# Stage 2 of an attention and expert kernel as two 64-row halves of the TensorE array, summed by VectorE

## The chip, the cores and the metric

The kernel runs on one core of one Trainium2 chip. The time is device microseconds of one execution; the kernel before took 500.78 us (median of 3 runs, 500.53 to 500.85). Engines are called PE (TensorE matmuls), PEld (TensorE's weight loads), DVE (VectorE), ACT (ScalarE) and SP (the engine that issues most DMAs).

## The reference

An attention with a small state (8 batches, 8 heads, 512 tokens and 32 state rows of 64 numbers) in both directions, and then a bilinear expert network over all 8 x 544 = 4352 rows:

```python
scores = scale * np.matmul(x, state.transpose(0, 1, 3, 2))
a = softmax(scores); xread = np.matmul(a, state)
scores2 = scale * np.matmul(state, x.transpose(0, 1, 3, 2))
a2 = softmax(scores2); sread = np.matmul(a2, x)
x = concat([xread, sread])          # 8 x 544 rows of 512
h = (x @ w1) * (x @ w2)             # 1024 wide
return (h @ w3) @ w_out             # 512 wide
```

## The kernel before, in words

A prologue turns the float64 weights into f32 and multiplies w3 by w_out once, so that the network's second half is a single product with `wo` (1024 x 512). Both factors of the large products are split into a high and a low fp32r part, and three products (low x high, high x high, high x low) stand for one f32 product.

For each batch there are two stages on PE:

- **Stage 1** (`stage1`, L297 to L311), 8 steps `ft` of 12 full-array matmuls of 512 columns (L306). Each step fills a pair of PSUM banks with x @ w1 and x @ w2 for 128 of the 1024 columns. `hidden` (L287) evacuates it: ACT copies one bank (L290), DVE multiplies it by the other (L291), ACT and DVE split the result into `g_hi` and `g_lo` (L96, L97).
- **Stage 2** (`stage2`, L320), 4 tiles `tt` of 128 tokens. Each sums 8 x 3 = 24 full-array matmuls (L316) into one bank; `store` (L326) lets ACT copy the bank to a tile `tmp` (L329) and then issues the output DMA from ACT's own queue (L331).

After the first stage 2 tile of batches 1 to 6 stand the **side steps** of the next batch (`side_steps`, L335): two weight products `w[0]`, `w[1]`, the score product, `read_state` of this batch (L242, and its scaling on DVE, L247), and two more weight products `w[2]`, `w[3]`. Weight and score products are the per-head matmuls at L146: 64 rows by 32 columns of the array, f32, eight places of the array one after the other. Each weight product is split into `sw_hi` (ACT, L96) and `sw_lo` (DVE, L97). Batch 7 has only `read_state` there. The softmax of the next batch runs on DVE and ACT meanwhile (L186 to L227).

At the end `state_rows` (L492) does the same network for the 256 state rows: 8 steps with pieces of w1 and w2 that ACT and DVE split on the way (`grp_z`), and 2 stage 2 tiles.

PSUM has eight banks. The pool `ps_o` holds two single banks (`bank()`), the pool `ps_2` three pairs (`two_banks()`); each request takes the buffer that was requested longest ago and waits until its last reader is done. Before the change the stage 2 tiles and `read_state` take single banks; stage 1, weight products and scores take pairs.

PE's and SP's instructions stand in the order in which the code issues them. ACT's and DVE's are ordered by the tile framework after the prologue, with `store` and `hidden` at high priority. Every engine works its own queue in order, and ACT's queue holds its casts and copies as well as its output DMAs.

Of the kernel before, what the change touches and what calls it, by code (L numbers as in the profile page):

```python
# [27 lines left out]
ALU = mybir.AluOpType  # L28
AX = mybir.AxisListType
P = 128  # L30
# [8 lines left out]
def attn_bilinear_kernel(  # L39
# [10 lines left out]
    nc = tc.nc  # L50
    B, _, NT, H, D = x_s.shape
    S = NT * P
    NP = H // 2
    NS = st.shape[3]
    KT = H * NS // P
    FT, DO = w34_k.shape[0], out.shape[2]
# [3 lines left out]
    PER = P // NS  # L60
# [23 lines left out]
    wo = {part: const.tile([P, FT, DO], F32R, name=f"wo_{part}") for part in ("hi", "lo")}  # L84
    const.tile([P, 32], F32, name="pad_1")

    def bank():
        return ps_o.tile([P, NF], F32, name="ps_o")

    def two_banks():  # L90
        return ps_2.tile([P, 2, NF], F32, name="ps_2")

    def split(hi, lo, src):

        return (
            nc.scalar.copy(out=hi, in_=src),  # L96
            nc.vector.tensor_tensor(out=lo, in0=src, in1=hi.bitcast(F32), op=ALU.subtract),  # L97
        )
# [51 lines left out]
    def load_x(b):  # L150
        sts[b] = att.tile([P, NP, NS], F32, name="st")
        nc.sync.dma_start(out=sts[b], in_=st[b])
        x_tiles[b] = att.tile([P, NP, S], F32, name="x_d", bufs=1)
        nc.sync.dma_start(out=x_tiles[b], in_=x_d[b])

    def load_tokens(b):
        token_tiles[b] = att.tile([P, NT, H, D], F32, name="x_s", bufs=1)
        nc.sync.dma_start(out=token_tiles[b], in_=x_s[b])
# [135 lines left out]
    def new_g():  # L294
        return [main.tile([P, NF], F32R, name=f"g_{part}", bufs=FT) for part in ("hi", "lo")]
# [17 lines left out]
    def project(ps, gs, tt, ft):  # L313
        g_hi, g_lo = (g[:, tt * P:(tt + 1) * P] for g in gs[ft])
        for k, (g, w) in enumerate(((g_hi, "lo"), (g_hi, "hi"), (g_lo, "hi"))):
            nc.tensor.matmul(  # L316
                ps[:, :DO], g, wo[w][:, ft, :], start=(ft == 0 and k == 0), stop=(ft == FT - 1 and k == 2)
            )

    def stage2(gs, tt, dests):  # L320
        ps = bank()
        for ft in range(FT):
            project(ps, gs, tt, ft)
        store(ps, dests)

    def store(ps, dests):  # L326
        o = main.tile([P, NF], F32, name="tmp", bufs=4)[:, :DO]
        with tc.high_priority():
            stored[:] = [nc.scalar.copy(out=o, in_=ps[:, :DO])]  # L329
        for (dest, first, n), queue in zip(dests, cycle((nc.scalar, nc.sync))):  # L330
            queue.dma_start(out=dest, in_=o[first:first + n])  # L331

# [2 lines left out]
    def side_steps(b):  # L335


        if b == B:
            return [[reads[b - 1]], [], [], []]
        scores, reads[b], a2 = attention_steps(b)  # L340
        w = sw_steps(b)
        softmax = scores()
        first = partial(islice, softmax, 3)
        if b == 1:
            def rest():

                with tc.issue_after(stored[0].ins):
                    yield from softmax

            return [[first], [reads[0], w[0], w[1]], [], [rest], [w[2], w[3]], []]  # L350

        product = partial(islice, softmax, 1)
        return [[w[0], w[1], product, reads[b - 1], w[2], w[3], lambda: softmax], [], [], []]

    def run(steps):
        for step in steps:
            for _ in step() or ():
                pass

    def batch_stage2(b, gs):  # L360
        side = side_steps(b + 1)
        for tt in range(NT):
            stage2(gs, tt, [(out[b, tt * P:(tt + 1) * P], 0, P)])
            run(side[tt])
        if b + 1 < B:
            load_tokens(b + 1)
        if b + 2 < B:
            load_x(b + 2)


    with tc.tile_pool(name="pro", bufs=2) as pro:
# [43 lines left out]
        gs, acc, early = [], [], range(2)  # L415
# [10 lines left out]
        pair = two_banks()  # L426
# [53 lines left out]
        for tt in range(NT):  # L480
            dests = [(out[0, tt * P:(tt + 1) * P], 0, P)]
            if tt in early:
                store(acc[tt], dests)
            else:
                stage2(gs, tt, dests)
            run(side[tt])
# [5 lines left out]
    def state_rows():  # L492
        n = B * NS

        sr = late.tile([P, NP, 2, n], F32R, name="grp_sr")
        split(sr[:, :, 1], sr[:, :, 0], sread)
        gs = []
        for ft in range(FT):
            quarter, c = divmod(ft * P, NQ)
            ps = two_banks()  # L500
            for i in range(2):
                wh, wl = (late.tile([P, NP * P], F32R, name=f"grp_z{q}", bufs=3) for q in range(2))
                as_w = lambda t: t.rearrange("p (j f) -> p j f", j=NP)
                split(as_w(wh), as_w(wl), w_sb[:, quarter, i, :, c:c + P])
                for kt in range(NP):
                    ks = slice(kt * P, (kt + 1) * P)
                    nc.tensor.matmul(ps[:, i], wh[:, ks], sr[:, kt], start=(kt == 0), stop=False)  # L507
                    nc.tensor.matmul(ps[:, i, :n], wl[:, ks], sr[:, kt, 1], start=False, stop=(kt == NP - 1))  # L508
            gs.append([g[:, :n] for g in new_g()])
            sums = main.tile([P, 2, n], F32, name="tmp", bufs=4)  # L510
            halves = ps.rearrange("p i (half n) -> p i half n", n=n)
            nc.scalar.copy(out=sums, in_=halves[:, :, 1])
            nc.vector.tensor_tensor(out=sums, in0=sums, in1=halves[:, :, 0], op=ALU.add)
            nc.vector.tensor_tensor(out=sums[:, 0], in0=sums[:, 0], in1=sums[:, 1], op=ALU.mult)
            split(*gs[-1], sums[:, 0])
        for tt in range(n // P):
            stage2(gs, tt, [(out[tt * PER + q, S:], q * NS, NS) for q in range(PER)])


    for b in range(1, B):  # L520
        gs = []
        for ft in range(FT):
            stage1(b, ft, gs)
        batch_stage2(b, gs)
    with tc.issue_after(last_split[0].ins), tc.issue_after(last_split[1].ins):
        state_rows()
# [44 lines left out]
```

## Time and profile before

| what | value |
|---|---|
| median of 3 runs | 500.78 us |
| span of the profiled execution | 498.4 us |
| PE busy | 492.3 us, 99% |
| PEld busy | 362.8 us, 73% |
| DVE busy | 285.7 us, 57% |
| ACT busy | 219.3 us, 44% |
| mean granted TensorE clock | 0.999 |

The span runs from the first to the last instruction of the profiled execution; that execution has no time of its own on record besides its span. Matmuls overlap in the pipeline, so the mean duration of one is longer than the distance from one to the next; the distance is read from the chain of work that ended last, as the length of a piece over its count. A plain f32 matmul of the code stands in the trace as two matmul records, an fp32r one as one. An entry like `[0.70 <-DVE sw_lo L97]` says that the engine sat idle for 0.70 us before the instruction and which one ended the wait. Of the groups by line, the columns are the count, the busy time in all, the mean of one in ns, and the idle time before them.

### The profile page before, as it was taken

The numbers are of one execution on the slowest core, as the hardware profiler recorded it, in microseconds if no ns is written. First come the engines' busy times: TensorE is split into PE (matmuls) and PEld (weight loads), VectorE is DVE, ScalarE is ACT, GpSimd is POOL, SyncE is SP. The second block draws the span as 40 slices with busy tenths as digits, with TensorE's granted clock in tenths as the row PEclk, the third lists the DMA queues.
The fourth block names the chain that finished last, engine by engine and source line by source line (L and its number), as shares of the span: only waits on it lengthen the run. The fifth ranks groups of instructions, "written<-read, shape, count | busy, mean of one in ns | idle before, by whom it ended". The sixth has DMA issues, their size and how long they took to land.

```text
span 498.4 us, 7562 instructions
## 1 busy us (share of the span) xinstructions
PE 492.3 (99%) x3054; PEld 362.8 (73%) x3054; DVE 285.7 (57%) x394; ACT 219.3 (44%) x325; POOL 0.2 (0%) x4
## 2 busy tenths in 40 slices
PE   8999999999999999999999999999999999999996
PEld 6444467767867886788678867886788678888885
DVE  5669896772539343934393539354934493530780
ACT  4777884443444244334333434243424342431650
POOL 0000000000000000000000000000000000000000
PEclk9999999999999999999999999999999999999999
DMA  8996962013400350035003500350035003301001
GB/s 343 364 380 237 364 264 33 11 47 80 181 22 19 79 189 23 20 79 188 21 27 76 185 22 27 77 184 22 26 78 183 22 26 78 93 24 49 21 1 42
DMA packets 52323, 52.41 MB, mean 105 GB/s; under 512 B 42304, under 2 KB 43328, under 8 KB 47680
## 3 DMA queue, kind: packets, MB, share of 16 engines
q1 hardware_dynamic: 47488, 43.27, 26.3%
q10 hardware_dynamic: 4800, 8.65, 4.6%
q8 instruction: 24, 0.39, 0.3%
q14 instruction: 11, 0.09, 0.1%
HBM read 38.27 MB, written 8.91 MB: 95 GB/s over the span
## 4 chain that ended last, share of the span: by engine, by line
PE 95%; DVE 2%; ACT 2%; DMA 1%; issue 0%; DVEq 0%
PE ps_o L316 38%; PE ps L306 35%; PE ps L146 7%; PE ps L507 3%; PE ps_o L402 3%; PE ps_o L389 3%; PE ps L389 3%; PE ps L508 2%; PE ps_o L242 1%; DMA raw<-in_w_k_dram 1%; ACT ulps L125 0%; ACT w_sb L117 0%; ACT wo_hi L96 0%; DVE w L133 0%; DVE work L204 0%; DVE wo_lo L97 0%
## 5 line engine op out<-in xcount | busy, mean ns | idle before, releaser
L316 PE MATMUL ps_o<-wo_lo,g_hi 128*128 128x512 f32 x272 | 107.0, 394 | 0.0
L316 PE MATMUL ps_o<-wo_hi,g_hi 128*128 128x512 f32 x272 | 106.0, 390 | 0.0
L316 PE MATMUL ps_o<-wo_hi,g_lo 128*128 128x512 f32 x272 | 105.9, 389 | 0.0
L306 PE MATMUL ps<-at_lo,sw_hi 128*128 128x512 f32 x256 | 100.1, 391 | 0.0
L306 PE MATMUL ps<-at_hi,sw_lo 128*128 128x512 f32 x256 | 99.6, 389 | 0.0
L306 PE MATMUL ps<-at_hi,sw_hi 128*128 128x512 f32 x256 | 99.6, 389 | 0.0
L291 DVE TENSOR_TENSOR tmp<-tmp,ps 128x512 f32<-128x512 f32 x64 | 43.9, 687 | 77.0 <-ACT tmp L290 76.9
L97 DVE TENSOR_TENSOR g_lo<-tmp,g_hi 128x512 fp32r<-128x512 f32 (+1 forms) x72 | 47.5, 661 | 41.7 <-ACT g_hi L96 41.6
L96 ACT CAST g_hi<-tmp 128x512 fp32r<-128x512 f32 (+1 forms) x72 | 43.1, 599 | 53.6 <-DVE tmp L291 48.8
L290 ACT COPY tmp<-ps 128x512 f32<-128x512 f32 x64 | 37.7, 589 | 62.8 <-PE ps L306 52.2
L316 PEld LDWEIGHTS ps_o<-wo_lo,g_hi 128*128 128x128 f32 x272 | 51.0, 188 | 18.0 <-issue 7.5
L316 PEld LDWEIGHTS ps_o<-wo_hi,g_lo 128*128 128x128 f32 x272 | 51.1, 188 | 10.8
L316 PEld LDWEIGHTS ps_o<-wo_hi,g_hi 128*128 128x128 f32 x272 | 51.1, 188 | 10.3
L97 DVE TENSOR_TENSOR sw_lo<-ps,sw_hi 128x1024 fp32r<-128x1024 f32 (+1 forms) x34 | 38.4, 1155 | 32.8 <-ACT sw_hi L96 32.8
L306 PEld LDWEIGHTS ps<-at_lo,sw_hi 128*128 128x128 f32 x256 | 48.1, 188 | 10.9 <-issue 1.1
L306 PEld LDWEIGHTS ps<-at_hi,sw_hi 128*128 128x128 f32 x256 | 48.1, 188 | 10.2 <-issue 0.2
L306 PEld LDWEIGHTS ps<-at_hi,sw_lo 128*128 128x128 f32 x256 | 48.1, 188 | 10.0
L329 ACT COPY tmp<-ps_o 128x512 f32<-128x512 f32 x34 | 19.8, 583 | 76.1 <-PE ps_o L316 76.1
L96 ACT CAST sw_hi<-ps 128x1024 fp32r<-128x1024 f32 (+1 forms) x34 | 31.7, 967 | 14.3 <-PE ps L146 14.2
L146 PE MATMUL ps<-w_sb,st 64*32 64x512 f32 (+1 forms) x544 | 31.6, 572 | 0.0
L402 PE MATMUL ps_o<-w_sb,w 128*128 128x512 f32 x64 | 28.5, 599 | 0.1
L402 PEld LDWEIGHTS ps_o<-w_sb,w 128*128 128x128 f32 x64 | 11.8, 190 | 15.9 <-issue 13.8
(65 smaller groups left out, 417.9 us busy)
## 6 DMA issues: line engine op xcount, KB each, us to landing
raw<-in_w_k_dram SPq DMA_DIRECT2D x8, 1024.0 KB, 6.6
x_d<-in_x_d_dram SPq DMA_DIRECT2D x8, 1024.0 KB, 7.1
raw<-in_w_dram SPq DMA_DIRECT2D x8, 1024.0 KB, 6.3
x_s<-in_x_s_dram SPq DMA_DIRECT2D x8, 1024.0 KB, 5.4
out_dram<-tmp ACTq DMA_DIRECT2D x32, 256.0 KB, 2.0
raw<-in_w3t_dram SPq DMA_DIRECT2D x4, 1024.0 KB, 7.2
a_t<-work SPq DMA_DIRECT2D x96, 32.0 KB, 1.9
sread<-turned SPq DMA_DIRECT2D x128, 4.0 KB, 1.7
```

The source lines that it names most:

```text
L96: nc.scalar.copy(out=hi, in_=src),
L97: nc.vector.tensor_tensor(out=lo, in0=src, in1=hi.bitcast(F32), op=ALU.subtract),
L146: nc.tensor.matmul(ps[j * NS:(j + 1) * NS, q], sts[b][rows, j], moving(rows, j), start=True, stop=True)
L290: nc.scalar.copy(out=a_sb[:, :n], in_=ps[:, 0, :n])
L291: nc.vector.tensor_tensor(out=a_sb[:, :n], in0=a_sb[:, :n], in1=ps[:, 1, :n], op=ALU.mult)
L306: nc.tensor.matmul(ps[:, i], w[:, kt, c:c + P], a[:, kt], start=(k == 0), stop=(k == 3 * KT - 1))
L316: nc.tensor.matmul(ps[:, :DO], g, wo[w][:, ft, :], start=(ft == 0 and k == 0), stop=(ft == FT - 1 and k == 2))
L329: stored[:] = [nc.scalar.copy(out=o, in_=ps[:, :DO])]
L389: nc.tensor.matmul(w34_ps[i][:, :DO], chunks[k][:, DO + i * P:DO + (i + 1) * P], w_out[k], start=(k == 0), stop=(k == FT - 1),)
L402: nc.tensor.matmul(w34_ps[i][:, :DO], w3s[i][:, k * P:(k + 1) * P], w_out[k], start=(k == 0), stop=(k == FT - 1))
L507: nc.tensor.matmul(ps[:, i], wh[:, ks], sr[:, kt], start=(kt == 0), stop=False)
L508: nc.tensor.matmul(ps[:, i, :n], wl[:, ks], sr[:, kt, 1], start=False, stop=(kt == NP - 1))
```

## The change

Stage 2 of batches 1 to 7 and of the state rows is computed by `stage2_rows`. Each of its matmuls becomes two: one over the upper 64 rows of the contraction (array rows 0 to 63), one over the lower 64. Both have all 128 columns. The two halves sum in two different banks, 24 matmuls into each. `store` lets ACT copy the first bank as before and then has DVE add the second to the copy; the DMA follows the add. Batch 0 keeps its stage 2. The banks come from `sums_of`: tiles 0, 2 and 3 of a batch take a pair of `ps_2`, tile 1 takes both single banks of `ps_o`; of the state rows' two tiles the first takes the single banks, the second a pair.

```diff
+    def stage2_rows(gs, tt, dests, sums):
+        for ft in range(FT):
+            g_hi, g_lo = (g[:, tt * P:(tt + 1) * P] for g in gs[ft])
+            for k, (g, w) in enumerate(((g_hi, "lo"), (g_hi, "hi"), (g_lo, "hi"))):
+                for r, ps in enumerate(sums):
+                    rows = slice(r * P // 2, (r + 1) * P // 2)
+                    nc.tensor.matmul(
+                        ps[:, :DO], g[rows], wo[w][rows, ft, :],
+                        start=(ft == 0 and k == 0), stop=(ft == FT - 1 and k == 2),
+                    )
+        store(sums[0], dests, sums[1])
+
-    def store(ps, dests):
+    def store(ps, dests, other=None):
         o = main.tile([P, NF], F32, name="tmp", bufs=4)[:, :DO]
         with tc.high_priority():
             stored[:] = [nc.scalar.copy(out=o, in_=ps[:, :DO])]
+            if other is not None:
+                nc.vector.tensor_tensor(out=o, in0=o, in1=other[:, :DO], op=ALU.add)
...
+    def sums_of(tt):
+        if tt == 1:
+            return bank(), bank()
+        pair = two_banks()
+        return pair[:, 0], pair[:, 1]
+
     def batch_stage2(b, gs):
         side = side_steps(b + 1)
         for tt in range(NT):
-            stage2(gs, tt, [(out[b, tt * P:(tt + 1) * P], 0, P)])
+            stage2_rows(gs, tt, [(out[b, tt * P:(tt + 1) * P], 0, P)], sums_of(tt))
             run(side[tt])
...
-            stage2(gs, tt, [(out[tt * PER + q, S:], q * NS, NS) for q in range(PER)])
+            stage2_rows(gs, tt, [(out[tt * PER + q, S:], q * NS, NS) for q in range(PER)], sums_of(1 - tt))
```

On ACT, this stands after the first stage 2 tile of batch 3 before the change, from that tile's copy to the cast of the next batch's `at_hi`. In brackets are the engines and DMA lanes that an instruction waits for.

```order
L329 COPY tmp<-ps_o 128x512 [waits PE_49,Activation_49]
L331 DMA out_dram<-tmp 128x512 [waits DMAHW6_49,Activation_49]
L96 CAST sw_hi<-ps_1987 128x1024 [waits PE_49]
L96 CAST sw_hi<-ps_2000 128x1024 [waits PE_49]
L96 CAST sw_hi<-ps_2075 128x1024 [waits PE_49]
L196 ACTIVATE e_2106,sum_2107<-ps_2013,m_2103 128x512 [waits DVE_49]
L196 ACTIVATE e_2106,sum_2107<-ps_2013,m_2103 128x512
L96 CAST sw_hi<-ps_2088 128x1024 [waits PE_49]
L207 ACTIVATE work<-work 128x1024 [waits DMAHW2_49,DMAHW5_49,DMAHW1_49,DVE_49]
L329 COPY tmp<-ps_o 128x512 [waits PE_49]
L331 DMA out_dram<-tmp 128x512 [waits DMAHW7_49,Activation_49]
L96 CAST at_hi<-work 128x1024 [waits DVE_49]
```

And after the change, at the same place (copy and DMA are at L343 and L347 there):

```order
L343 COPY tmp<-ps_2161 128x512 [waits PE_49,Activation_49]
L347 DMA out_dram<-tmp 128x512 [waits DMAHW6_49,DVE_49]
L96 CAST sw_hi<-ps_2214 128x1024 [waits PE_49]
L96 CAST sw_hi<-ps_2227 128x1024 [waits PE_49]
L96 CAST sw_hi<-ps_2302 128x1024 [waits PE_49]
L196 ACTIVATE e_2333,sum_2334<-ps_2240,m_2330 128x512 [waits DVE_49]
L196 ACTIVATE e_2333,sum_2334<-ps_2240,m_2330 128x512
L96 CAST sw_hi<-ps_2315 128x1024 [waits PE_49]
L207 ACTIVATE work<-work 128x1024 [waits DMAHW3_49,DMAHW4_49,DMAHW0_49,DVE_49]
L96 CAST at_hi<-work 128x1024 [waits DVE_49]
L343 COPY tmp<-ps_o 128x512 [waits PE_49,Activation_49]
L347 DMA out_dram<-tmp 128x512 [waits DMAHW1_49,DVE_49]
```

The first tile's DMA keeps its place ahead of the casts, but waits for DVE's add in place of ACT's own copy. The second tile's copy and DMA have moved behind the cast of `at_hi`. On DVE the first tile's add (L345) stands ahead of the `sw_lo` subtractions, and the adds of tiles two to four stand together behind the last step of the softmax (L227); in batch 7 they stand behind the split of the state rows (`grp_sr`).

On PE, this stands at the start of a batch's second stage 2 tile before the change (batch 3; `ps_o_2146` is the tile's bank, and the row ahead is the last of the side steps' per-head matmuls):

```order
L146 MATMUL ps_2_2088<-w_sb_90,st_1795 32x512 x7
L316 MATMUL ps_o_2146<-wo_lo_94,g_hi_1812 128x512 [waits Activation_49]
L316 MATMUL ps_o_2146<-wo_hi_93,g_hi_1812 128x512
L316 MATMUL ps_o_2146<-wo_hi_93,g_lo_1813 128x512
L316 MATMUL ps_o_2146<-wo_lo_94,g_hi_1832 128x512
L316 MATMUL ps_o_2146<-wo_hi_93,g_hi_1832 128x512
```

And after the change, at the same place; `ps_o_2373` takes the upper half's sum, `ps_o_2374` the lower half's (the 128x512 is the shape of the output, not of the weights):

```order
L146 MATMUL ps_2_2315<-w_sb_90,st_1997 32x512 x7
L334 MATMUL ps_o_2373<-wo_lo_94,g_hi_2014 128x512
L334 MATMUL ps_o_2374<-wo_lo_94,g_hi_2014 128x512 [waits DVE_49]
L334 MATMUL ps_o_2373<-wo_hi_93,g_hi_2014 128x512
L334 MATMUL ps_o_2374<-wo_hi_93,g_hi_2014 128x512
L334 MATMUL ps_o_2373<-wo_hi_93,g_lo_2015 128x512
L334 MATMUL ps_o_2374<-wo_hi_93,g_lo_2015 128x512
```

Every matmul has become two that follow each other. Before, the tile's first matmul waited for ACT's copy of the first tile; now the lower half's first one waits for DVE: its bank is the one that `read_state` used in the same batch and that the scaling (L247) reads. (Before, that was the bank of the third tile.)

## The prediction

> **What bounds the kernel now.** I read the page's busy times first, then the chain that ended last, then the timeline of one batch (the one from 365 to 416 us).
>
> ```profile
> PE 492.3 (99%) x3054; PEld 362.8 (73%) x3054; DVE 285.7 (57%) x394; ACT 219.3 (44%) x325; POOL 0.2 (0%) x4
> PE 95%; DVE 2%; ACT 2%; DMA 1%; issue 0%; DVEq 0%
> L316 PE MATMUL ps_o<-wo_lo,g_hi 128*128 128x512 f32 x272 | 107.0, 394 | 0.0
> ```
>
> TensorE (PE) is busy for 99% of the span and is 95% of the chain; stage 2 (L316) is one of its two large parts. Whatever PE loses or gains per matmul, or waits at a stage's edge, arrives at the end one for one. The 394 ns of a stage 2 matmul is a latency: matmuls overlap in the pipeline. The rate stands in the chain (columns: start, length, what, how many):
>
> ```profile
> 15.24 1.72 PE ps_o L389 x4
> 388.42 5.44 PE ps_o L316 x24
> 393.86 2.74 PE ps L146 x48
> 396.60 1.03 PE ps_o L242 x64
> 397.63 1.91 PE ps L146 x32
> 399.53 16.59 PE ps_o L316 x72
> 416.12 21.76 PE ps L306 x96
> 494.44 0.59 ACT tmp L329
> ```
>
> A full-array fp32r matmul of 512 columns costs 5.44/24 = 0.2267 us, in stage 2 as in stage 1 (21.76/96 = 0.2267). A plain f32 one (L389) costs 1.72/4 = 0.430 us.
>
> **Part 1: 720 full-array matmuls become 720 pairs.** Batches 1 to 7 have 7 x 4 tiles of 24 matmuls (672), the state rows 2 x 24 (48). Each becomes two matmuls of 64 rows and 128 columns. No row of this trace has that shape in fp32r. The nearest one is the per-head product (L146), 64 rows by 32 columns in f32, eight places of the array at once (first number: start):
>
> ```profile
> 394.25 0.15 PEld L146 LDWEIGHTS ps<-w_sb,st 64*32 64x32 f32 x8 [0.28 <-issue]
> 394.67 0.15 PEld L146 LDWEIGHTS ps<-w_sb,st 64*32 64x32 f32 x8 [0.28 <-issue]
> 395.10 0.15 PEld L146 LDWEIGHTS ps<-x_d,st 64*32 64x32 f32 x8 [0.28 <-issue]
> ```
>
> A round of eight comes every 0.43 us, exactly the 0.430 us of one f32 matmul on the whole array. So both row halves and all column groups run together, into two banks, and packing costs nothing; nor does it gain anything per round. I take the same for the pair: 0.2267 us, a change of 0. The bounds: 0.430/2 = 0.215 us, half of what an f32 record takes for the same 512 columns, as the best a pair could do (720 x -0.0117 = -8.4 us); upward, an extra 0.008 us a pair for issuing twice as many matmuls (half of the 1.03/64 = 0.016 us in which L242 issues one), +5.8 us.
>
> A rule speaks for a small loss here. The Trainium skill, "TensorE: Matmul & The Clock Gate", Part 3, measured speedup against the span model, has each further tile add about 4 ns to a packed group; by that estimate the sum would be 720 x 4 ns = 2.9 us higher. The 0.43 us of a round of eight shows no such charge once rounds follow each other, so I keep 0.
>
> **Part 2: the array changes its division more often.** Stage 1 and stage 2 now share the full array. After the change PE switches from full array to row halves ahead of a batch's first stage 2 tile and back after its fourth. What a switch costs: L146 x48 is six rounds of 0.430 = 2.58 us, but takes 2.74: 0.16 us when entered from the full array. L316 x72 is 72 x 0.2267 = 16.32 us, but takes 16.59: 0.27 us when entered from L146. I take the middle, 0.22 us. The switches around the side steps exist already. New ones: 7 x 2, and one ahead of the state rows' stage 2: 15 x 0.22 = +3.3 us (0 if halves and full array need no switch, 15 x 0.27 = 4.1).
>
> **Part 3: VectorE adds, and ScalarE's queue waits for it.** The 30 adds read one bank and write a 128x512 tile, as L291 does. The place where this matters is after the first tile, at the side steps of the next batch (batches 1 to 6):
>
> ```profile
> L291 DVE TENSOR_TENSOR tmp<-tmp,ps 128x512 f32<-128x512 f32 x64 | 43.9, 687 | 77.0 <-ACT tmp L290 76.9
> 393.95 0.59 ACT L329 COPY tmp<-ps_o 128x512 f32<-128x512 f32 x1 [3.48 <-PE ps_o L316]
> 394.57 0.34 ACTq L331 DMA_DIRECT2D out_dram<-tmp  x1
> 394.99 1.93 ACT L96 CAST sw_hi<-ps 128x1024 fp32r<-128x1024 f32 x2 [0.45 <-PE ps L146]
> 396.03 2.36 DVE L97 TENSOR_TENSOR sw_lo<-ps,sw_hi 128x1024 fp32r<-128x1024 f32 x2 [4.83 <-ACT sw_hi L96]
> 398.44 0.18 PEld L146 LDWEIGHTS ps<-w_sb,st 64*32 64x32 f32 x16 [0.70 <-DVE sw_lo L97]
> PEld ps L146 <- DVE sw_lo L97: 4.2, 6, 0.7
> ```
>
> Today the output DMA is issued 0.03 us after the copy ends (394.54 to 394.57), and the first cast of the side steps starts 0.42 us after the issue (394.99). After the change the same DMA stands in ScalarE's queue behind a wait for VectorE's add: 0.69 us plus one more handover of 0.03 us. Queued behind it are both sw_hi casts; behind those, VectorE's two sw_lo subtractions (396.03 to 398.39); behind these, PE, whose fourth weight product (398.44) needs the bank that the second subtraction frees. The last row says that this is the releaser in all six batches, with no slack. So the 0.72 us passes to PE whole: 6 x 0.72 = +4.3 us. The third weight product (397.63 in the chain) would then wait for the first subtraction too (half of the 2.36 us on, at about 397.2, + 0.72), but that lies inside the same 0.72.
>
> The pair of the first tile must be free for the score product, which starts at 395.53. The add ends at 394.57 + 0.69 = 395.26, so 0.27 us remains; VectorE is idle there (4.83 us before 396.03). I put it at nothing; without that cover it would be a few tenths a batch.
>
> **Part 4: the second tile takes both single banks.** One of them is what read_state's scaling (L247) reads:
>
> ```profile
> 399.46 0.25 DVE L247 TENSOR_TENSOR scaled<-ps_o,sum 128x128 f32<-128x128 f32 x1
> 399.46 0.50 PE L316 MATMUL ps_o<-wo_lo,g_hi 128*128 128x512 f32 x1
> 399.81 0.40 PE L316 MATMUL ps_o<-wo_hi,g_hi 128*128 128x512 f32 x1
> ```
>
> Today the second tile's first matmul starts at 399.46 and its second at 399.81, so 0.35 - 0.23 = 0.12 us of the entry is paid there anyway. The lower half now waits until 399.71, plus a handover. Its second matmul can then come 0.23 us later, at about 399.97, not at 399.81: 0.15 us each in 7 batches = +1.1 us (0 to 0.3 each: 0 to 2.1).
>
> **Part 5: the end and the covered places.** The last tile's copy (494.44) is followed by an add before its DMA: +0.7 us, on the path.
>
> ```profile
> 412.25 1.24 DVE L227 STREAM_TRANSPOSE work<-e 128x1024 f32<-128x1024 f32 x1
> 416.16 0.59 ACT L329 COPY tmp<-ps_o 128x512 f32<-128x512 f32 x1 [4.60 <-PE ps_o L316]
> 418.88 0.59 ACT L290 COPY tmp<-ps 128x512 f32<-128x512 f32 x1 [2.13 <-PE ps L306]
> 458.39 1.23 DVE L97 TENSOR_TENSOR grp_sr<-sread,grp_sr 128x1024 fp32r<-128x1024 f32 x1 [13.34 <-ACT grp_sr L96]
> 462.87 0.69 DVE L97 TENSOR_TENSOR grp_z<-w_sb,grp_z 128x512 fp32r<-128x512 f32 x1 [3.25 <-ACT grp_z L96]
> 465.13 0.23 PE ps L507
> ```
>
> Tiles two to four: their adds stand behind L227, which ends at 413.5. Copy, add and issue in a row are 0.59 + 0.69 + 0.42 = 1.7 us a tile: the adds end near 414.2, 415.9 and 417.6, ahead of stage 1's first copy (418.88). Cost 0; if that cover were gone, the late part would fall on ScalarE, which waits there anyway. In batch 7 the same three stand behind grp_sr, which ends at 459.6. The third add ends near 463.7 and the state rows' fourth weight piece, ready today at 463.56, comes about 0.9 us later; PE takes it at 465.13. Cost 0, with 0.7 us to spare.
>
> **The sum.** 0 + 3.3 + 4.3 + 1.1 + 0.7 = +9.4 us on the span:
>
> ```profile
> core 0: 498.4 us, clock 0.999
> ```
>
> The profiled execution gives 498.4 + 9.4 = 507.8 us. The median of the runs (500.78) lies 2.4 us above its span, so I forecast 510.2 us. Side costs at their low ends are 0 + 4.3 + 0 + 0.7 = 5.0, at their high ends 4.1 + 4.3 + 2.1 + 0.7 = 11.2 us: 505.8 to 512.0 us for this case.
>
> **The rivals.**
>
> *The weight change is hidden.* A fp32r matmul has 0.2267 us where an f32 one shows 0.215 per half. If the difference is what changing the weights costs a row group, and the other half streams on meanwhile, a pair takes 0.215:
>
> ```profile
> 402.13 0.39 PE L316 MATMUL ps_o<-wo_hi,g_lo 128*128 128x512 f32 x1
> 402.13 0.19 PEld L316 LDWEIGHTS ps_o<-wo_lo,g_hi 128*128 128x128 f32 x1
> 402.36 0.39 PE L316 MATMUL ps_o<-wo_lo,g_hi 128*128 128x512 f32 x1
> ```
>
> Against it: the next weights begin to load when the current matmul starts (both 402.13) and take 0.19 of the 0.23 us, so the load is already beside the stream; and each half still changes its own weights between its own matmuls. For it: 0.012 us per matmul is unexplained. With the side costs as summed: 510.2 - 8.4 = 501.8 us. The Trainium skill, "TensorE: Matmul & The Clock Gate", Part 3, the mechanism, says that a weight load overlaps with running matmuls only where their row groups differ. That would favour this rival; the two rows at 402.13 do not bear it out for the full array.
>
> *The same, and switches are free* (the other side): 500.8 - 8.4 + 5.0 = 497.4 us, faster. It decides where the pair gains more than the side costs take: below 0.2267 - 5.0/720 = 0.220 us a pair.
>
> *The pair costs more*, by up to 0.008 us for issue: 510.2 + 5.8 = 516.0 us.
>
> *The halves don't run side by side in fp32r*, by their streams or by their two weight loads (2 x 0.19 = 0.38 us a pair): 720 x 0.153 = +110 us, near 620 us. The rounds of eight in 0.43 us, with eight loads in 0.15 us, speak against it, but in f32 with 32 columns.
>
> **How the numbers follow.** Chances: forecast 0.53; hidden with the side costs 0.17; hidden with free switches 0.12; pair dearer 0.12; serial 0.06. A measurement of this kernel can tell about 0.2%, 1.0 us, from no change: faster means below 499.8, slower above 501.8. The fourth case (497.4) is faster, with 0.01 from the edge of the hidden case: 0.13. The hidden case ends on the border, so I split it: same 0.09. The rest is slower: 0.78. The range leaves out the serial case (0.06) and the fast one (0.12): from 499.5, the hidden case with its side costs some 2 us lower, to 517.0.
>
> **What would show it.** Chain: x48 groups of stage 2 at 5.44 us (pair 0.2267) or 5.16 (0.215); 10.9 would be serial. The cast after the first copy starting 0.7 us later against PE, and the fourth weight product waiting for it in six batches. A gap of some 0.2 us at stage 1's first matmul. The prediction is wrong if stage 2's pairs run well below 0.220 us, if PE does not wait for sw_lo longer than today, or if stage 2 takes longer than 5.7 us a tile.

## The result

| | before | after |
|---|---|---|
| median of 4 runs (lowest to highest), us | 500.78 (500.53 to 500.85) | 518.17 (517.09 to 518.43) |
| ratio, 95% interval | | 1.0342 (1.0327 to 1.0356) |
| span of the profiled execution, us | 498.4 | 516.5 |
| PE busy, us | 492.3 | 501.1 |

The change makes the kernel 17.4 us slower. I had forecast slower by 9.4 us, with 517.0 us as the upper end of the range; the direction was right, the size was not.

The page after the change: the busy times, the shares of the chain by engine, and the group of copies that matters (behind the bar: busy us, mean ns of one, idle time before them and its releaser).

```profile
PE 501.1 (97%) x3774; PEld 364.9 (71%) x3774; DVE 303.1 (59%) x424; ACT 217.0 (42%) x325; POOL 0.2 (0%) x4
PE 54%; DVE 20%; DMA 7%; ACT 6%; SPq 6%; issue 4%; ACTq 1%; DVEq 0%
L343 ACT COPY tmp<-ps 128x512 f32<-128x512 f32 x22 | 12.9, 586 | 88.4 <-DMA a_t<-work 38.1
```

PE's share of the chain has fallen from 95% to 54%. SP's queue (SPq) stands in it now and DMA has grown from 1% to 7%, which no part of the prediction foresaw. The third row names the DMAs: ScalarE stood idle for 38.1 us ahead of the copies of stage 2's tiles (L343), until DMAs called `a_t<-work` had landed. The waits of the trace (sum us, how many, longest) say which of them reached PE:

```profile
ACT tmp L343 <- DMA a_t<-work: 38.1, 6, 7.5
PEld ps L146 <- DVE sw_lo L97: 8.9, 12, 0.9
PEld ps L306 <- DVE tmp L345: 7.0, 6, 2.3
```

The second row was 4.2 us in 6 waits before; it is the side steps of Part 3. The third row is new: stage 1 (L306) waits once in each of six batches, up to 2.3 us, for stage 2's add (L345).

I then cut PE's time into the stages of each batch, from the start of each stage's first matmul to the start of the next stage's, in both traces (us):

| stage | before | after | difference in all |
|---|---|---|---|
| prologue and batch 0, to batch 1's stage 1 | 119.29 | 119.75 | 0.5 |
| first stage 2 tile, 7 batches | 5.53 | 5.69 | 1.1 |
| side steps, 6 batches | 5.67 | 6.36 | 4.1 |
| tiles two to four, batches 1 to 6 | 16.45 to 16.49 | 16.85 to 16.87 | 2.3 |
| the same, batch 7 | 16.45 | 17.24 | 0.8 |
| stage 1, batch 1 | 21.76 | 21.85 | 0.1 |
| stage 1, batches 2 to 7 | 21.76 | 22.80, 24.23, 22.84, 22.85, 22.86, 22.85 | 7.9 |
| state rows up to their stage 2 | 22.60 | 22.80 | 0.2 |
| state rows' stage 2, to the end | 15.12 | 16.27 | 1.2 |

These sum to 18.1 us, the difference of the spans. The largest row is stage 1 of batches 2 to 7. The change does not touch stage 1, and I had put its cover at no cost. A row runs up to the next stage's first matmul, so what a change of division costs ahead of that matmul stands in the row of the stage before it: the 0.1 us of batch 1's stage 1, which comes out of a whole-array stage 2, is the start of the change into the first tile's halves.

**Where stage 1's time goes.** The chain of the changed kernel at the entry to batch 7's stage 1 (start, length, what, how many):

```profile
433.12 1.91 DMA a_t<-work
435.11 0.34 ACTq L347
435.54 0.60 ACT tmp L343
436.16 0.70 DVE tmp L345
436.90 16.64 PE ps L306 x72
```

Read it from below. Stage 1's third step starts at 436.90 and has waited for the fourth tile's add. The add waited for the fourth tile's copy, that for ScalarE's output DMA of the third tile (L347), and that DMA for an `a_t` move on SP's queue, which landed at 435.03. No data join the two DMAs. The timeline shows how long the third tile's output had been ready (in brackets: idle time before, and its releaser):

```profile
427.85 10.50 SPq L170 DMA_DIRECT2D a_t<-work  x16
428.83 0.59 ACT L343 COPY tmp<-ps 128x512 f32<-128x512 f32 x1 [2.97 <-DVE tmp L345]
429.44 0.69 DVE L345 TENSOR_TENSOR tmp<-tmp,ps 128x512 f32<-128x512 f32 x1 [1.09 <-ACT tmp L343]
435.11 0.34 ACTq L347 DMA_DIRECT2D out_dram<-tmp  x1
435.54 0.59 ACT L343 COPY tmp<-ps 128x512 f32<-128x512 f32 x1 [6.13 <-DMA a_t<-work]
436.90 0.50 PE L306 MATMUL ps<-at_lo,sw_hi 128*128 128x512 f32 x1 [0.52 <-DVE tmp L345]
```

The third tile's add ends at 430.13; its DMA is issued at 435.11, 4.98 us later, and everything behind it on ScalarE waits. (It is 5.0 us in five of the six batches and 6.4 in the other.) The compiled order with its waits says why. Each DMA of SP and ACT is given one of eight completion counters (DMAHW0 to 7), and waits until the DMA that had the same counter before has landed. On ACT, tiles three and four of this batch (row number first):

```
277 L343 COPY tmp<-ps_4041 128x512 [waits PE_49,Activation_49]
278 L347 DMA out_dram<-tmp 128x512 [waits DMAHW5_49,DVE_49]
279 L343 COPY tmp<-ps_4094 128x512 [waits PE_49,Activation_49]
280 L347 DMA out_dram<-tmp 128x512 [waits DMAHW7_49,DVE_49]
```

On SP, the ninth of the sixteen moves that stand ahead of them in the program's order has the third tile's counter; the moves take the counters in turn:

```
272 L170 DMA a_t<-work 32x8x32 [waits DMAHW3_49]
273 L170 DMA a_t<-work 32x8x32 [waits DMAHW4_49]
274 L170 DMA a_t<-work 32x8x32 [waits DMAHW5_49]
```

SP issues sixteen moves in 10.50 us, so the ninth starts to be issued some 5.2 us after 427.85 (433.12 in the chain), and its landing frees the counter. In the kernel before, tiles three and four both have DMAHW7 at this place, and the `a_t` moves skip that counter: the third tile's DMA waits for a move of `sread` that stands ahead of them all on SP, the fourth's for the third's. So the doubled matmuls have changed the order in which the framework hands out counters, and an output DMA has been tied to a transfer that it has nothing to do with. (That it is the matmuls, and not the adds or the banks, follows from two of the experiments: with the adds and banks but whole-array matmuls the counters are those of before, and with the halves but no add the tie is there.)

### The profile page after: what moved, and what is told of

It reads as the page before. It is cut to its first block, busy times and chain, and to the rows that moved or that the text cites. A ratio compares the mean times of both kernels' runs of the same rounds, so it can differ in the third digit from the quotient of the medians.

```text
span 516.5 us, 9073 instructions
## 1 busy us (share of the span) xinstructions
PE 501.1 (97%) x3774; PEld 364.9 (71%) x3774; DVE 303.1 (59%) x424; ACT 217.0 (42%) x325; POOL 0.2 (0%) x4
## 4 chain that ended last, share of the span: by engine, by line
PE 54%; DVE 20%; DMA 7%; ACT 6%; SPq 6%; issue 4%; ACTq 1%; DVEq 0%
PE ps L306 28%; PE ps L334 11%; SPq L170 6%; PE ps_o L316 4%; DVE sw_lo L97 4%; DMA raw<-in_w_k_dram 3%; PE ps L529 3%; PE ps_o L424 3%; DMA a_t<-work 2%; PE ps_o L334 2%; DVE tmp L345 2%; PE ps L146 2%; DVE work L186 2%; ACT tmp L343 2%; DVE work L204 2%
## 5 line engine op out<-in xcount | busy, mean ns | idle before, releaser
L306 PE MATMUL ps<-at_lo,sw_hi 128*128 128x512 f32 x256 | 101.7, 397 | 4.5 <-DVE tmp L345 4.5
L306 PE MATMUL ps<-at_hi,sw_lo 128*128 128x512 f32 x256 | 99.8, 390 | 0.0
L306 PE MATMUL ps<-at_hi,sw_hi 128*128 128x512 f32 x256 | 99.8, 390 | 0.0
L334 PE MATMUL ps<-wo_lo,g_hi 64*128 64x512 f32 x352 | 95.4, 391 | 0.0
L334 PE MATMUL ps<-wo_hi,g_lo 64*128 64x512 f32 x352 | 94.6, 387 | 0.0
L334 PE MATMUL ps<-wo_hi,g_hi 64*128 64x512 f32 x352 | 94.5, 386 | 0.0
L291 DVE TENSOR_TENSOR tmp<-tmp,ps 128x512 f32<-128x512 f32 x64 | 43.6, 683 | 33.0 <-ACT tmp L290 25.0
L306 PEld LDWEIGHTS ps<-at_lo,sw_hi 128*128 128x128 f32 x256 | 48.1, 188 | 19.8 <-DVE tmp L345 7.0
L334 PEld LDWEIGHTS ps<-wo_lo,g_hi 64*128 64x128 f32 x352 | 53.4, 184 | 8.4 <-issue 2.5
L345 DVE TENSOR_TENSOR tmp<-tmp,ps 128x512 f32<-128x512 f32 x22 | 15.1, 687 | 74.6 <-ACT tmp L343 74.6
L334 PEld LDWEIGHTS ps<-wo_hi,g_lo 64*128 64x128 f32 x352 | 53.4, 184 | 6.5
L334 PEld LDWEIGHTS ps<-wo_hi,g_hi 64*128 64x128 f32 x352 | 53.5, 185 | 5.9
L306 PEld LDWEIGHTS ps<-at_hi,sw_lo 128*128 128x128 f32 x256 | 48.1, 188 | 10.3
L306 PEld LDWEIGHTS ps<-at_hi,sw_hi 128*128 128x128 f32 x256 | 48.1, 188 | 9.8 <-issue 0.2
L290 ACT COPY tmp<-ps 128x512 f32<-128x512 f32 x64 | 37.3, 584 | 40.2 <-PE ps L306 28.4
L343 ACT COPY tmp<-ps 128x512 f32<-128x512 f32 x22 | 12.9, 586 | 88.4 <-DMA a_t<-work 38.1
L334 PE MATMUL ps_o<-wo_lo,g_hi 64*128 64x512 f32 x128 | 39.6, 401 | 0.2 <-DVE scaled L247 0.2
L334 PE MATMUL ps_o<-wo_hi,g_hi 64*128 64x512 f32 x128 | 38.5, 392 | 0.0
```

What stands on the lines that cost most here:

```text
L290: nc.scalar.copy(out=a_sb[:, :n], in_=ps[:, 0, :n])
L291: nc.vector.tensor_tensor(out=a_sb[:, :n], in0=a_sb[:, :n], in1=ps[:, 1, :n], op=ALU.mult)
L306: nc.tensor.matmul(ps[:, i], w[:, kt, c:c + P], a[:, kt], start=(k == 0), stop=(k == 3 * KT - 1))
L334: nc.tensor.matmul(ps[:, :DO], g[rows], wo[w][rows, ft, :], start=(ft == 0 and k == 0), stop=(ft == FT - 1 and k == 2),)
L345: nc.vector.tensor_tensor(out=o, in0=o, in1=other[:, :DO], op=ALU.add)
```

## The experiments

Each edit is one of the changed kernel, unless another is named. Where queues are given to `stage2_rows`, it passes them on to `store`, whose loop takes them in place of `(nc.scalar, nc.sync)`.

**First tile's output on SP's queue.** Part 3 held that ScalarE's queue waits for the add because the output DMA stands in it.

```diff
-            stage2_rows(gs, tt, [...], sums_of(tt))
+            stage2_rows(gs, tt, [...], sums_of(tt), (nc.sync,) if tt == 0 else None)
```

> Only the output DMA of each batch's first tile goes to SP's queue, where nothing waits behind it, in place of ACT's. Theory (the add holds up ACT's queue and with it the side steps): the side steps of six batches go from 6.36 back to 5.67 us, 6 x 0.69 = 4.1 us less than the changed kernel: 514.1 us. Rival (the row halves themselves slow PE, and the queue is only late alongside): no change, 518.2 us.

Measured: 514.13 us (513.18 to 515.08), ratio to the kernel before 1.0271 (1.0256 to 1.0287). Its waits:

```profile
ACT tmp L343 <- DMA a_t<-work: 37.8, 6, 6.8
PEld ps L146 <- DVE sw_lo L97: 4.2, 6, 0.7
PEld ps L306 <- DVE tmp L345: 6.5, 6, 1.6
```

The second row is back at the 4.2 us of the kernel before and the side steps at 5.67 us; stage 1's wait stays. Part 3's mechanism is shown, at 4.0 us.

**The other tiles' output on GpSimd's queue.** The same edit with `(nc.gpsimd,) if tt else None`. In the compiled order these DMAs have counters of their own (DMASW0 to 7), which no move on SP shares.

> Only the output DMAs of tiles two to four of each batch go to POOL's queue in place of ACT's. Theory (ACT's DMA of tile three waits for a DMA lane that an a_t move still holds, tile four's copy and add come late, and stage 1's third step waits for their bank pair): stage 1 of batches 2 to 7 goes from 22.8 us or more to 21.9 us, 6.1 us in all: 512.1 us. Rival (stage 1 waits for the add because VectorE is late, whatever the queue): 518.2 us.

Measured: 511.58 us (511.35 to 512.15), ratio 1.0223 (1.0206 to 1.024). In its chain stage 1 is one piece again:

```profile
261.24 10.88 PE ps L334 x96
272.12 22.01 PE ps L306 x96
```

22.01 us in each of batches 2 to 7, not 22.80 to 24.23, and the fourth tile's copy and add run at once, when PE has finished the tile:

```profile
424.94 0.59 ACT L343 COPY tmp<-ps 128x512 f32<-128x512 f32 x1 [4.44 <-PE ps L334]
425.56 0.69 DVE L345 TENSOR_TENSOR tmp<-tmp,ps 128x512 f32<-128x512 f32 x1 [2.45 <-ACT tmp L343]
```

The side steps keep their 6.36 us. So the wait for the counter costs 518.17 - 511.58 = 6.6 us. The 22.01 - 21.76 = 0.25 us that is left in stage 1 is division: 0.16 us of the change out of the halves and 0.09 of the next one into them, as batch 1's 21.85 shows, which has only the second.

**Both queues.** `(nc.gpsimd,) if tt else (nc.sync,)`.

> Both moves: first tile's output DMA on SP, the other three on POOL. Theory: 518.2 - 4.1 - 6.1 = 508.0 us, with the switches of the array's division (2.9), the second tile's bank wait (about 2) and the longer end (1) left. Rival (the row halves themselves): 518.2 us.

Measured: 508.49 us (507.68 to 508.58), ratio 1.0155 (1.014 to 1.017). The two costs nearly add up: 4.0 + 6.6 = 10.6 us from the two alone, 9.7 us measured together. 7.7 us over the kernel before remain. The chain shows pairs and stage 1 without a gap between them:

```profile
259.95 10.88 PE ps L334 x95
270.83 22.01 PE ps L306 x96
```

**Two banks and the add, but whole-array matmuls.** This takes the halves away and keeps everything that surrounds them: 24 matmuls a tile go to the two banks in turn, and VectorE adds the banks.

```diff
-                for r, ps in enumerate(sums):
-                    rows = slice(r * P // 2, (r + 1) * P // 2)
-                    nc.tensor.matmul(
-                        ps[:, :DO], g[rows], wo[w][rows, ft, :],
-                        start=(ft == 0 and k == 0), stop=(ft == FT - 1 and k == 2),
-                    )
+                n = 3 * ft + k
+                nc.tensor.matmul(
+                    sums[n % 2][:, :DO], g, wo[w][:, ft, :], start=n < 2, stop=n >= 3 * FT - 2
+                )
```

> The two banks, the add and ACT's queue stay as in the changed kernel, but the matmuls are whole-array ones again, the even ones summing in one bank and the odd ones in the other. ACT's order of copies and DMAs is then that of the kernel before, except for the wait for the add. Theory: the side steps still cost 4.1 us, the second tile's bank wait 1 to 2, the end 1; no switches and no wait at stage 1's third step: 507 us (506 to 508.5). Rival (the division of the array is what costs): 501 to 503 us.

Measured: 506.44 us (506.1 to 506.5), ratio 1.0116 (1.0101 to 1.0131). The side steps take the same 6.36 us, but stage 1 is 21.76 us in all batches:

```profile
270.64 21.76 PE ps L306 x96
292.40 5.45 PE ps L333 x24
```

The adds and their DMAs on ScalarE are all there, and the counter's wait is not. In this kernel's compiled order tiles three and four have DMAHW7 again, as before the change, and the moves skip it. So the add as such does not bring the wait.

**The add left out.** My theory before this run was that the add carries the lateness of ScalarE's queue into stage 1.

```diff
-            if other is not None:
-                nc.vector.tensor_tensor(out=o, in0=o, in1=other[:, :DO], op=ALU.add)
```

> The changed kernel without VectorE's add: the lower half's sum is left out of the output, and ACT's DMAs follow ACT's own copies again. ACT's order and the DMA lanes stay like the changed kernel's. Theory (the lane makes tile four's copy late, and it is the add behind it that carries the lateness over the edge; the side steps wait for the add): side steps at 5.67 us, stage 1 at about 22.0 us, only switches and the second tile's bank wait left: 507 us. Rival (the lane wait stalls stage 1 by itself): about 512 us.

Measured: 514.61 us (513.77 to 514.92), ratio 1.027 (1.0253 to 1.0287). The theory fell. The side steps are back at 5.67 us, but stage 1 of batches 2 to 6 takes 22.66, 23.28, 22.71, 26.02 and 22.78 us; only batch 7's has the 22.01 us without a wait:

```profile
ACT tmp L343 <- DMA a_t<-work: 48.3, 6, 8.6
PEld ps L306 <- DVE tmp L291: 6.4, 5, 2.5
```

```profile
332.16 0.34 ACTq L345 DMA_DIRECT2D out_dram<-tmp  x1
332.87 0.59 ACT L290 COPY tmp<-ps 128x512 f32<-128x512 f32 x1 [4.47 <-DMA a_t<-work]
```

The output DMA waits for a move's counter here too, and without the add it is stage 1's own first copy (L290) that stands behind it on ScalarE. PE then waits one step later, for the banks that this copy and VectorE's L291 free. What makes the wait is the counter that the DMA gets and the queue that it stands in; the add only decides who meets it first.

**One half after the other.** The two loops are exchanged: a tile's 24 upper-half matmuls first, then its 24 lower-half ones. It asks whether the halves run side by side because they are neighbours in the queue.

```diff
-        for ft in range(FT):
-            g_hi, g_lo = (g[:, tt * P:(tt + 1) * P] for g in gs[ft])
-            for k, (g, w) in enumerate(((g_hi, "lo"), (g_hi, "hi"), (g_lo, "hi"))):
-                for r, ps in enumerate(sums):
-                    rows = slice(r * P // 2, (r + 1) * P // 2)
+        for r, ps in enumerate(sums):
+            rows = slice(r * P // 2, (r + 1) * P // 2)
+            for ft in range(FT):
+                g_hi, g_lo = (g[:, tt * P:(tt + 1) * P] for g in gs[ft])
+                for k, (g, w) in enumerate(((g_hi, "lo"), (g_hi, "hi"), (g_lo, "hi"))):
```

> The same matmuls, banks and stores, but of each tile the 24 upper halves come first and then the 24 lower ones, so that neighbours in the queue have the same array rows. Theory (two halves share the time only when they stand side by side in PE's queue): a tile takes 2 x 24 x 0.227 = 10.9 us, 30 tiles more by 5.44 us each: 518 + 163 = 681 us. Rival (PE lets the lower halves start early): between 518 and 600 us.

Measured: 638.9 us in one run, between the two expectations. Its timeline at the crossing of a tile's halves:

```profile
146.28 0.39 PE L334 MATMUL ps<-wo_lo,g_hi 64*128 64x512 f32 x1
146.50 0.39 PE L334 MATMUL ps<-wo_hi,g_hi 64*128 64x512 f32 x1
146.73 0.39 PE L334 MATMUL ps<-wo_hi,g_lo 64*128 64x512 f32 x1
146.74 0.61 PE L334 MATMUL ps<-wo_lo,g_hi 64*128 64x512 f32 x2
147.07 0.50 PE L334 MATMUL ps<-wo_hi,g_hi 64*128 64x512 f32 x2
147.30 0.49 PE L334 MATMUL ps<-wo_hi,g_lo 64*128 64x512 f32 x2
```

A half alone takes 0.23 us (146.28, 146.50, 146.73), as long as the whole array or a pair: rows that stand unused save nothing. Only at the crossing do two stand in a row (x2): the last upper ones run beside the first lower ones. Of the 681 - 639 = 42 us that the expectation is missed by, 6.4 are stage 1's, which takes 22.01 us here: stage 2's tiles are so long that the third tile's DMA finds its counter all but free (0.1 us of wait). The other 36 us over about 45 crossings are 0.8 us each, three to four matmuls.

**The third tile on the whole array, the rest in halves.** From the kernel with both queues; the third tile uses one bank and no add. It puts two more changes of division into each of seven batches.

```diff
+            if tt == 2:
+                ps = two_banks()[:, 0]
+                for ft in range(FT):
+                    project(ps, gs, tt, ft)
+                store(ps, dests, None, (nc.gpsimd,))
+            else:
+                stage2_rows(gs, tt, dests, sums_of(tt), (nc.gpsimd,) if tt else (nc.sync,))
```

> Both queue moves, and the third tile of each batch is computed on the whole array in one bank without an add. It sits between two tiles in halves, so PE changes the array's division twice more in each of 7 batches. Theory (a change costs about 0.2 us): 508.5 + 14 x 0.2 = 511.2 us, although a quarter of the pairs and adds is gone. Rival (changes of division are free, halves cost by themselves): 508.5 us or a little less.

Measured: 511.65 us (511.29 to 511.73), ratio 1.0215 (1.0199 to 1.023); 3.2 us more than without the whole tile, 0.23 us for each of 14 changes by the medians. In the trace a tile between two changes takes 5.69 us, whichever kind it is, where 24 times 0.2267 is 5.44: 0.25 us more.

```profile
260.73 5.69 PE ps L316 x24
266.41 5.69 PE ps L334 x48
272.10 22.01 PE ps L306 x96
```

**Whole-array matmuls in two banks, first tile's output on SP.** The fourth experiment with the first one's edit: no halves, no wait in ScalarE's queue, no counter's wait. What is left is the price of the banks and the adds.

> Whole-array matmuls summed in two banks with the add, and the first tile's output DMA on SP's queue. The kernel differs from the one before only in banks, adds and one queue. Theory (what the whole-array form still pays is the queue's 4.1 us): 506.4 - 4.1 = 502.3 us, and 6.2 us below the halves with both queue moves, of which the switches are 15 x 0.2 = 2.9 us and the rest the second tile's lower half. Rival (another wait comes up in the freed place): 504 us or more.

Measured: 502.19 us (501.75 to 502.65), ratio 1.0026 (1.0015 to 1.0037):

```profile
267.96 21.76 PE ps L306 x96
289.72 5.44 PE ps L333 x24
295.16 2.74 PE ps L146 x48
300.83 5.75 PE ps_o L333 x24
```

Every stage but the second tile and the end is at its time from before the change.

## Why the prediction was right in direction and short in size

The medians divide the 17.4 us (each a difference of two kernels): the first tile's DMA behind the add 4.0 (518.17 - 514.13); the counter's wait 6.6 (518.17 - 511.58), both together 9.7 (518.17 - 508.49); the halves themselves 6.3 (508.49 - 502.19); the banks and adds 1.5 (502.19 - 500.74, the kernel before beside that run). 9.7 + 6.3 + 1.5 = 17.5. Of the 6.3, 0.9 is a longer prologue of the profiled run (120.16 us for 119.30), which differs so much from kernel to kernel without a cause that I know; the rest is the changes of division (3.7) and the lower half's late end (about 0.25 in each of seven batches), both below.

**Part 1, the pair costs what the whole matmul costs: right.** The timeline of the changed kernel within a tile:

```profile
403.91 0.39 PE L334 MATMUL ps<-wo_lo,g_hi 64*128 64x512 f32 x2
404.14 0.39 PE L334 MATMUL ps<-wo_hi,g_hi 64*128 64x512 f32 x2
404.36 0.39 PE L334 MATMUL ps<-wo_hi,g_lo 64*128 64x512 f32 x2
404.59 0.39 PE L334 MATMUL ps<-wo_lo,g_hi 64*128 64x512 f32 x2
```

Each row is a pair, and three pairs take 0.68 us, 0.227 each; 48 pairs take 10.88 us in the chain, 0.2267 each. All rivals about the pair fall: hidden weights (0.215), an issue charge (0.235), and halves one after the other, which the kernel that orders them so measures at 638.9 us, where I had put near 620. Two halves whose weight loads fall in different rows run no faster than the whole array. The further 4 ns a tile that the Trainium skill's "TensorE: Matmul & The Clock Gate", Part 3, gives a packed group does not show in this steady stream. Neither does the gain of the rival that, by the prediction, the rule on weight loads in the same part of the Trainium skill's page would favour. Why a matmul takes 0.2267 us and not 0.215 stays open.

**Part 2, 15 changes of division at 0.22 us: right, a little small.** A change costs 0.25 us: the first matmul behind it comes 0.09 late (21.85 for 21.76 in batch 1's stage 1), and the stage behind it takes 0.16 more (5.69 for 5.53 in the first tile, 22.01 for 21.85 in stage 1 without the counter's wait). Fifteen are about 3.7 us against 3.3. The mixed kernel gives 0.23 by the medians.

**Part 3, ScalarE's queue waits for the add: right.** 4.1 us in the trace and 4.0 us by experiment, against 4.3.

**Part 4, the second tile waits for L247: too small, 2.5 us for 1.1.** Tiles two to four cost 0.38 us more in six batches and 0.79 in batch 7; 0.09 of each is the change of division into stage 1. The two banks alone, with whole-array matmuls, cost 0.06 us (16.53 for 16.47) in the six. The rest comes with the halves: the second tile takes 5.98 us in pairs (in the kernel with the other tiles' output on GpSimd's queue), where it takes 5.75 with the whole array.

```profile
204.34 5.98 PE ps_o L334 x48
```

The prediction had the lower half start late and then run level with the upper one. The timeline shows otherwise. In the kernel with both queues the second tile's upper half starts at 203.63 and its lower half at 203.94, beside the upper half's second matmul, and it stays one matmul behind up to the fourth tile's end:

```profile
270.22 0.39 PE L334 MATMUL ps<-wo_hi,g_hi 64*128 64x512 f32 x1
270.45 0.39 PE L334 MATMUL ps<-wo_hi,g_lo 64*128 64x512 f32 x1
270.76 0.50 PE L306 MATMUL ps<-at_lo,sw_hi 128*128 128x512 f32 x1
271.10 0.40 PE L306 MATMUL ps<-at_hi,sw_hi 128*128 128x512 f32 x1
```

The lower half's last matmul (270.45) has no partner, so a short wait at the second tile's start costs a whole matmul, 0.23 us. (The steps of 0.31 and 0.34 us behind it, for 0.23, are the change of division.) In batch 7 a queue was missed. There the side steps are short, and VectorE has the first tile's add ahead of L247:

```profile
459.94 0.69 DVE L345 TENSOR_TENSOR tmp<-tmp,ps 128x512 f32<-128x512 f32 x1 [1.82 <-ACT tmp L343]
460.55 0.28 DVE L247 TENSOR_TENSOR scaled<-ps_o,sum 128x128 f32<-128x128 f32 x1
460.88 0.18 PEld L334 LDWEIGHTS ps_o<-wo_lo,g_hi 64*128 64x128 f32 x1 [0.51 <-DVE scaled L247]
```

PE's weight load waits 0.51 us for L247. The 0.47 us that batch 7 pays in the last experiment too (16.92 for 16.45), without halves, agrees.

**Part 5, the end and the covered places: this step failed.** The end itself cost 1.2 us for 0.7: the add's 0.7, which the whole-array kernel keeps (15.82 for 15.12), 0.2 of the last change of division, and 0.3 between the last add and the end of this execution (3.7 us, 3.4 in the others). The failure is the sentence that puts tiles two to four at no cost, because copy, add and issue follow each other in 1.7 us a tile and end ahead of stage 1's first copy. It took each output DMA to be issued as soon as its add ends. In the runs the third tile's DMA waits 5.0 to 6.4 us for its counter, the fourth tile's copy and add wait behind it on ScalarE, and stage 1's third step needs their banks: 6.6 us by experiment. "If that cover were gone, the late part would fall on ScalarE, which waits there anyway" was wrong too: ScalarE does wait, but PE waits for the banks that ScalarE and VectorE free. By the trace that wait is 6.4 us (the 7.9 of stage 1 less six times 0.25). With it the sum of 9.4 comes to 15.8; 1.4 more in Part 4, 0.4 more in Part 2 and 0.2 less in Part 3 make 17.4, and 0.5 in the prologue and 0.3 at the end, which no part named, make 18.2 where the spans differ by 18.1. None of the prediction's signs of being wrong looked at stage 1 beyond its first matmul, so none pointed at this step; a tile above 5.7 us, one of them, came true for the second tile alone.

The rows that would have shown it were to be had: the counters stand in the compiled order of the changed kernel beside each DMA, and SP's moves with the same number stand ahead of them. Reading the order for who stands behind whom on one engine was not enough; a wait named there for a counter ties two queues together.

Batch 3's stage 1 takes 24.23 us where the others take 22.8. SP's moves were slower there:

```profile
219.45 11.88 SPq L170 DMA_DIRECT2D a_t<-work  x16
228.10 0.34 ACTq L347 DMA_DIRECT2D out_dram<-tmp  x1
```

11.88 us for sixteen, 1.4 us more than in the other timeline, and stage 1 is later by 1.4 us. It is one move, the fifth, that held SP for 2.01 us where the others take 0.6 (the chain has it at 222.10). What slowed it was not tried.

## What to carry to other kernels

Splitting the contraction of a matmul that already fills the array into row halves gained nothing here: the pair takes as long as the whole, each change of division costs about 0.25 us, and a half that starts late ends late by a whole matmul. A compute engine's queue is a bad place for an output DMA that may have to wait; before putting one there, look up in the compiled order which earlier DMA holds its completion counter, and what of that engine's work stands behind it. When a change alters the number of instructions, compare the counters of all DMAs near it, also of those that the diff does not touch.

## What the runs showed of the hardware that was not expected

- A matmul of one row half starts ahead of earlier ones of the other half: with all 24 upper matmuls queued first, about four lower ones of a tile run beside the last four upper ones (638.9 us, some 36 us less than without overlap). The Trainium skill's "TensorE: Matmul & The Clock Gate", Part 3, has matmuls start and end in the order of the program; the rows at 146.74 to 147.30, two matmuls in each 0.23 us, do not bear that out across row halves. Nor does it hold for PE there that every engine works its own queue in order, as I wrote of the kernel before.
- Two halves that have come one matmul apart stay so as long as halves follow: from 203.94 in the second tile to the fourth tile's end, where 0.23 us are lost.
- A change between whole array and row halves costs 0.25 us in either direction, 0.09 up to the first matmul behind it and 0.16 after that (0.23 on the mean of the mixed kernel's 14). That is about as much as one matmul of 512 columns.
